# Attention and max-of-three MLP on one core: products with v held back until step 8, identity products in the first steps

## The chip, the cores and the metric

The kernel runs on one core of a Trainium2 chip. The core's engines work side by side, each through its own row of instructions, and wait for one another by semaphores: TensorE (PE in the profile) multiplies matrices, VectorE (DVE), ScalarE (ACT) and GpSimd (POOL) work on vectors, and SyncE (SP) issues DMAs. The metric is the device time of one execution in microseconds (us), as the median of several runs.

## The reference

Four batches of eight heads of attention, 576 positions of 64 values each, with a bias that a small network computes from the distance of two positions; the result goes through a layer that takes the maximum of three products and multiplies it by an output matrix.

```python
scores = scale * np.matmul(q, k.transpose(0, 1, 3, 2))
x = (psi_rel / psi_i)[..., None]
bias = np.maximum(x @ w1 + b1, 0.0) @ w2
scores = scores + bias.transpose(2, 0, 1)[None, :, :, :]
scores = scores - np.max(scores, axis=-1, keepdims=True)
attn = np.exp(scores)
attn = attn / (np.sum(attn, axis=-1, keepdims=True) + 1e-09)
attn_out = np.matmul(attn, v)
...
x = attn_out.transpose(0, 2, 1, 3).reshape(B * S, H * D)
h = np.maximum(np.maximum(x @ w1, x @ w2), x @ w3)
out = h @ w_out
```

## The kernel before

Three parts follow one another. The first (`bias_stage`) computes the bias for all heads and writes it to DRAM (`bias_d`). The second is attention, the third the max layer and its output (`moe`). The order of all instructions is that of the Python code (`manual_schedule`), with no scheduler behind it.

Attention runs over 16 units, each a pair of heads of one batch. A unit has NS = 5 steps, t = 0 to 4: four blocks of 128 query rows for two heads, and a last one that holds the left-over 64 rows of both heads. There are 80 steps, n = 0 to 79, and five more without a front that empty the pipeline (the drain). A step does the following, in this order:

- `front(n)`: PE multiplies q and k into the score banks s (L237). There are two such banks (tag "s", `bufs=2`), one for each head, so the next front waits for DVE's shifts of this one.
- the queue of products with v: `pvq` holds closures, and step t takes 1, 3, 2, 2 or 2 of them, if there are any (L348 to L350). This is the place of the change.
- `shift` and `expo`: DVE adds the bias and takes the minimum of the negated scores (sn and nm, L247; the last step of a unit uses the table biasm), ACT takes exponentials and their sums (e and sm, L259).
- `norm(n - 1)`: DVE's reciprocals of the sums of the step before (rc, L269), and POOL multiplies by them (L272).
- `prep`, at t = 0 and 1: ACT and POOL split q and k of the next unit (kh, kl, qh, ql).
- `split_x`: DVE writes a finished group of the attention's result out of PSUM, as xhi and xlo (L330, L331).
- `flip(n - 5)`: PE transposes the probabilities of five steps ago by products with an identity (tp at L291, the left-over columns into lp at L300); ACT (L369, L370) and DVE (L372) copy them to et.
- at t = 1 and t = 4 of the flipped step, `queue_pv` puts a group into the queue. It has five pairs of products (L320), one pair for each block of keys, the fifth with the tile vl, and sums into one PSUM bank (tag "pv", `bufs=1`). The group of t = 0 and 1 has 256 columns, that of t = 2 to 4 has 320.

The first pair of a group calls `split_x` for whatever is finished, and then writes to the same bank that the group before it used, so it has to wait until DVE has read that bank out.

The first group is put into the queue at the end of step 6, and the steps take from it as soon as there is something: two pairs at step 7, two at step 8, one at step 9. From then on each unit takes 1 and 3 pairs of a 320-column group at t = 0 and t = 1; at t = 2 its last pair and the first pair of a 256-column group; and 2 and 2 more of that group at t = 3 and t = 4. After the last step what is left in the queue is taken in one go (L529 and L530), and the third part begins.

Step 0 is issued at the end of the first part, while its last bias blocks are on their way; the loads of the last bias tables (`load_bias`, tile biasm at L161 to L163) stand in SP's row behind the stores of these blocks.

Of the kernel before, what the change touches and what calls it, by code (L numbers as in the profile page):

```python
# [9 lines left out]
F32 = mybir.dt.float32  # L10
# [9 lines left out]
def kernel(  # L20
# [12 lines left out]
    nc = tc.nc  # L33
# [13 lines left out]
    psum = ctx.enter_context(tc.tile_pool(name="psum", bufs=1, space=PSUM))  # L47
# [13 lines left out]
    ident = const.tile([128, 128], F32, name="ident")  # L61
# [95 lines left out]
    def load_bias(hp, t):  # L157
        if t < NTQ:
            nc.sync.dma_start(out=bias_t[t], in_=bias_rows(128 * t, 128, 2 * hp, 0, S, 2))
        else:  # L160
            nc.sync.dma_start(out=bias_t[t][0:LEFT], in_=bias_rows(LB, LEFT, 2 * hp, 0, S))  # L161
            nc.sync.dma_start(out=bias_t[t][64:64 + LEFT, 0:LB], in_=bias_rows(LB, LEFT, 2 * hp + 1, LEFT, LB))
            nc.sync.dma_start(out=bias_t[t][64:64 + LEFT, LB:S], in_=bias_rows(LB, LEFT, 2 * hp + 1, 0, LEFT))  # L163
# [4 lines left out]
    NS = NTQ + 1  # L168

    TS = 2  # L170
    sched = [(un, t) for un in range(len(units)) for t in range(NS)]
    NSTEP = len(sched)
    LAG = NS

    class Attention:
# [99 lines left out]
        def flip(self, n):  # L275
# [27 lines left out]
                nc.tensor.transpose(lp[0:64], e2[:, LB:S], ident)  # L303
            return tps, (el[:, c0:c0 + m], lp[:, 0:m])

        def queue_pv(self, un, c0, w0, ea, el):
            hp, b = units[un]
            u = self.data[un]
            made = []

            def pair(c):
                def run():
                    if c == 0:
                        self.split_x()
                        made.append(psum.tile([128, w0], F32, tag="pv", bufs=1, name=f"pv{un}_{c0}"))
                    pv = made[0]
                    for h in range(2):
                        p = slice(64 * h, 64 * h + 64)
                        w, x = (u["vt"][:, c, h], ea[:, c, h]) if c < NTQ else (u["vl"][:, h], el)
                        nc.tensor.matmul(pv[p], lhsT=w, rhs=x, start=(c == 0), stop=(c == NTQ))  # L320
                    if c == NTQ:
                        self.done.append((pv, hp, slice(b * S + c0, b * S + c0 + w0)))
                return run

            self.wait = True
            self.pvq.extend(pair(c) for c in range(NTQ + 1))
# [9 lines left out]
        def step(self, n, more=None):  # L336
            m, f = n - 1, n - LAG
            nh = 0
            if n < NSTEP:
                un, t = sched[n]  # L340
                hp, b = units[un]
                if t == 0 and un + 2 < len(units):
                    self.load_qk(un + 2)
                if t == 3 and un:
                    self.load_v(un)
                nh = self.heads(n)
                self.front(n)
            for _ in range((1, 3, 2, 2, 2)[n % NS]):  # L348
                if self.pvq:
                    self.pvq.pop(0)()  # L350
            back = 0 <= f < NSTEP
            for h in range(nh):
                self.shift(n, h)
                self.expo(n, h)
            if more is not None:
                next(more, None)
            if n < NSTEP and b == B - 1 and hp + 1 < HP:
                load_bias(hp + 1, t)
            if 0 <= m < NSTEP:
                self.norm(m)  # L360
            if n < NSTEP and un + 1 < len(units):
                if t == 0:
                    self.splits = self.prep(un + 1)
                if t < 2:
                    next(self.splits)
            self.split_x()
            if back:
                tps, left = self.flip(f)
                nc.scalar.copy(*tps[0])  # L369
                nc.scalar.copy(*left)  # L370
                if len(tps) > 1:
                    nc.vector.tensor_copy(*tps[1])  # L372
            if back:
                un, t = sched[f]
                g = 0 if t < TS else 1
                w = 128 * TS if g == 0 else S - 128 * TS
                del self.st[f]
                if t in (TS - 1, NS - 1):
                    self.queue_pv(un, 128 * TS * g, w, *self.et)
# [115 lines left out]
    with tc.manual_schedule():  # L495
        nc.vector.memset(signm, 0x80000000)
        warm = const.tile([128, 256], F32, name="warm")
# [6 lines left out]
        n = 0  # L504
# [87 lines left out]
```

## Time and profile before

| | us |
|---|---|
| median of 3 runs | 646.84 (646.67 to 647.37) |
| the profiled execution | 644.86 |
| its span, first to last instruction | 643.1 |
| PE busy in the span | 606.8 (94%) |
| DVE busy | 372.2 (58%) |
| ACT busy | 297.5 (46%) |
| POOL busy | 167.6 (26%) |

The bias part lasts until about 53 us, attention until about 344, the third part until the end. Busy time is a mean over these parts, so stretches are read by themselves: a table of windows gives the busy time of each engine and the clock that was granted to PE (PEclk, 1.00 is 2.4 GHz and 0.50 is 1.2 GHz). In a row of the order of time, the number in brackets is how long the engine stood idle before the instruction, and behind the arrow is what ended that. Where an instruction waits for nothing, the price of work in a row is read from one start to the next.

### The profile page before, as it was taken

How to read it: one execution, taken by the hardware profiler on the slowest of the kernel's cores; microseconds unless marked ns; L12 is line 12 of the kernel's file. 1: busy time of each engine (PE TensorE's matmuls, PEld its weight loads, DVE VectorE, ACT ScalarE, POOL GpSimd, SP SyncE). 2: the span in 40 equal slices, each digit the busy share in tenths (PEclk: the TensorE clock that was granted, in tenths of full speed). 3: DMA queues.
4: the chain of work that ended last, by engine and by line, in shares of the span. 5: the costliest groups of instructions: out<-in, count | busy, mean ns of one | idle time of the engine just before them, and what ended most of it. 6: DMA issues, size and time to landing. Idle time of an engine off the chain costs nothing.

```text
span 643.1 us, 11440 instructions
## 1 busy us (share of the span) xinstructions
PE 606.8 (94%) x4248; PEld 459.6 (71%) x4248; DVE 372.2 (58%) x942; ACT 297.5 (46%) x791; POOL 167.6 (26%) x189
## 2 busy tenths in 40 slices
PE   8997899999999999999989999999999999999998
PEld 4335666666666666666657898989889898988886
DVE  7993566667766766676644474646646473233331
ACT  7985767777777787777641000000000001034443
POOL 3403655555565556556320000000000000000000
PEclk9996799999999999999999999999999999999999
DMA  6978313621372235400001121212212110001111
GB/s 177 287 243 291 87 51 116 193 60 53 90 218 71 60 94 153 133 20 19 22 32 34 34 67 51 76 36 66 65 34 97 34 66 0 1 34 66 66 65 67
DMA packets 47863, 55.16 MB, mean 86 GB/s; under 512 B 21952, under 2 KB 31424, under 8 KB 47808
## 3 DMA queue, kind: packets, MB, share of 16 engines
q1 hardware_dynamic: 47808, 54.43, 27.4%
q8 instruction: 34, 0.56, 0.4%
q14 instruction: 21, 0.17, 0.1%
HBM read 38.81 MB, written 15.61 MB: 85 GB/s over the span
## 4 chain that ended last, share of the span: by engine, by line
PE 85%; ACT 5%; DVE 5%; issue 3%; DMA 2%; POOL 0%; DVEq 0%; ACTq 0%
PE pv L320 14%; PE s L237 12%; PE tp L291 11%; PE h L464 8%; PE h L466 8%; PE h L465 8%; PE g L464 4%; PE g L466 4%; PE g L465 4%; PE o L490 4%; PE o L489 4%; PE o L488 4%; ACT bs L144 2%; DMA bias_d<-bs 2%; DVE hid L106 1%
## 5 line engine op out<-in xcount | busy, mean ns | idle before, releaser
L259 ACT ACTIVATE e<-sn,nm 128x576 f32<-128x576 f32 x144 | 110.8, 771 | 71.5 <-DVE nm L247 66.0
L272 POOL TENSOR_SCALAR e<-e,rc 128x576 f32<-128x576 f32 x144 | 105.7, 747 | 92.6 <-PE tp L291 65.4
L471 ACT COPY m<-h 128x512 f32<-128x512 f32 (+1 forms) x30 | 16.3, 544 | 206.1 <-PE h L466 180.9
L247 DVE CUSTOM_DVE_ANT_0 sn<-s,bias 128x576 f32<-128x576 f32 x128 | 91.7, 753 | 34.2 <-PE s L237 34.2
L320 PE MATMUL pv<-et,vt 128*64 128x320 f32 (+1 forms) x512 | 79.4, 420 | 23.1 <-DVE xlo L331 20.2
L466 PE MATMUL h<-xhi,wl 128*128 128x512 f32 (+1 forms) x240 | 88.3, 368 | 0.0
L464 PE MATMUL h<-xhi,wh 128*128 128x512 f32 (+1 forms) x240 | 88.3, 368 | 0.0
L465 PE MATMUL h<-xlo,wh 128*128 128x512 f32 (+1 forms) x240 | 88.2, 368 | 0.0
L291 PEld LDWEIGHTS tp<-ident,e 128*128 128x128 f32 x576 | 62.3, 142 | 33.8 <-issue 30.3
L291 PE MATMUL tp<-ident,e 128*128 128x128 f32 x576 | 81.3, 282 | 0.0
L372 DVE COPY et<-tp 128x512 f32<-128x512 f32 x64 | 44.2, 690 | 42.7 <-PE tp L291 40.7
L320 PEld LDWEIGHTS pv<-et,vt 128*64 128x64 f32 x512 | 30.4, 136 | 52.5 <-issue 35.7
L237 PE MATMUL s<-kh,qh 64*128 64x288 f32 (+1 forms) x288 | 62.3, 359 | 3.9 <-DVE nm L247 2.8
L237 PE MATMUL s<-kl,qh 64*128 64x288 f32 (+1 forms) x288 | 52.8, 309 | 0.0
L237 PE MATMUL s<-kh,ql 64*128 64x288 f32 (+1 forms) x288 | 51.6, 303 | 0.0
L369 ACT COPY et<-tp 128x512 f32<-128x512 f32 x80 | 45.8, 573 | 9.1 <-PE tp L291 9.1
L464 PEld LDWEIGHTS h<-xhi,wh 128*128 128x128 f32 x240 | 45.1, 188 | 6.2 <-issue 0.5
L443 DVE TENSOR_TENSOR hl<-ht,hh 128x128 fp32r<-128x128 f32 x108 | 23.4, 285 | 44.9 <-ACT hh L442 44.9
L465 PEld LDWEIGHTS h<-xlo,wh 128*128 128x128 f32 x240 | 45.0, 188 | 5.8
L466 PEld LDWEIGHTS h<-xhi,wl 128*128 128x128 f32 x240 | 45.0, 188 | 5.7
L472 DVE TENSOR_TENSOR m<-h,m 128x512 f32<-128x512 f32 (+1 forms) x30 | 19.1, 637 | 51.3 <-ACT m L471 51.3
L206 POOL TENSOR_TENSOR kl<-kr,kh 128x640 fp32r<-128x640 f32 x16 | 32.5, 2034 | 58.7 <-ACT kh L205 58.7
(77 smaller groups left out, 1051.5 us busy)
## 6 DMA issues: line engine op xcount, KB each, us to landing
bias_d<-bs SPq DMA_DIRECT2D x36, 295.5 KB, 5.0
bias<-bias_d SPq DMA_DIRECT2D x16, 576.0 KB, 4.0
w<-in_moe_w_dram SPq DMA_DIRECT2D x18, 512.0 KB, 3.5
qr<-in_qd_dram SPq DMA_DIRECT2D x16, 320.0 KB, 3.6
kr<-in_kd_dram SPq DMA_DIRECT2D x16, 320.0 KB, 3.8
out_dram<-ot SPq DMA_DIRECT2D x17, 256.0 KB, 2.0
vt<-in_v_dram SPq DMA_DIRECT2D x32, 128.0 KB, 2.5
w64o<-in_moe_w_out_dram SPq DMA_DIRECT2D x6, 512.0 KB, 3.2
```

Of the source, the lines that this page charges most:

```text
L206: nc.gpsimd.tensor_tensor(out=lo, in0=r, in1=hi.bitcast(F32), op=ALU.subtract)
L237: nc.tensor.matmul(ss[h][:, x, 0:HALF], lhsT=u[q][p, r], rhs=u[k][p, c:c + HALF], start=(j == 0), stop=(j == 2))
L247: nc.vector.tensor_tensor_reduce(out=sn.rearrange("p (a b) -> p a b", a=2), in0=st["s"][h][:, :, 0:HALF], in1=bt.rearrange("p (a b) -> p a ...
L259: nc.scalar.activation(st["e"][:, S * h:S * h + S], sn, ACTF.Exp, scale=-1.0, bias=nm, accum_out=st["sm"][:, h:h + 1])
L272: nc.gpsimd.tensor_scalar(out=e, in0=e, scalar1=rc[:, h:h + 1], scalar2=1.0, op0=ALU.mult, op1=ALU.mult)
L291: nc.tensor.transpose(tp[:, 128 * c:128 * c + 128], e2[:, k0:k0 + 128], ident)
L320: nc.tensor.matmul(pv[p], lhsT=w, rhs=x, start=(c == 0), stop=(c == NTQ))
L369: nc.scalar.copy(*tps[0])
L372: nc.vector.tensor_copy(*tps[1])
L464: nc.tensor.matmul(o, lhsT=hi[:, r], rhs=x, start=(c == 0), stop=False)
L465: nc.tensor.matmul(o, lhsT=hi[:, r], rhs=y, start=False, stop=False)
L466: nc.tensor.matmul(o, lhsT=lo[:, r], rhs=x, start=False, stop=(c == KDM - 1))
```

## The change

A pair is taken from the queue only from step n = LAG + TS + 1 = 8 on (LAG is 5, TS is 2). The steps 0 to 4 get a new method, `warm`, behind the front: four products of the identity with itself, 128 x 128, into the bank of lp, which nothing reads. Nothing else changes; the numbers 1, 3, 2, 2, 2 stay.

```diff
+        def warm(self, n):
+            w = psum.tile([128, 128], F32, tag="l", bufs=1, name=f"warm{n}")
+            for _ in range(4):
+                nc.tensor.matmul(w, lhsT=ident, rhs=ident, start=True, stop=True)
+
         def queue_pv(self, un, c0, w0, ea, el):
...
                 nh = self.heads(n)
                 self.front(n)
+            if n < NS:
+                self.warm(n)
             for _ in range((1, 3, 2, 2, 2)[n % NS]):
-                if self.pvq:
+                if self.pvq and n >= LAG + TS + 1:
                     self.pvq.pop(0)()
```

In the rows of order below, a line number of after is larger by 5 to 8 than that of before (L326 is L320, L336 and L337 are L330 and L331, L380 is L372).

PE, step 17 (t = 2 of the fourth unit), from the end of the front to the flip; pv_256 is the group of 320 columns, pv_0 the one of 256. Before:

```order
L237 MATMUL s_2_0_1639<-kh_1315,ql_1371 128x288
L237 MATMUL s_2_1_1640<-kh_1315,ql_1371 128x288
L320 MATMUL pv_256_1546<-et_1_1425,vl_82 64x320 x2
L320 MATMUL pv_0_1657<-et_0_1568,vt_1441 64x256 x2
L291 MATMUL tp_2_0_1677<-ident,e_1413 128x128 x4
L291 MATMUL tp_2_1_1682<-ident,e_1413 128x128 x4
L300 MATMUL lp_2_1687<-ident,e_1413 128x128
```

And after:

```order
L237 MATMUL s_2_0_1662<-kh_1335,ql_1394 128x288
L237 MATMUL s_2_1_1663<-kh_1335,ql_1394 128x288
L326 MATMUL pv_256_1620<-et_1_1447,vt_1215 64x320 x2
L326 MATMUL pv_256_1620<-et_1_1447,vl_82 64x320 x2
L291 MATMUL tp_2_0_1699<-ident,e_1433 128x128 x4
L291 MATMUL tp_2_1_1704<-ident,e_1433 128x128 x4
L300 MATMUL lp_2_1709<-ident,e_1433 128x128
```

The step now takes the last two pairs of one group; the first pair of the next group has moved to step 18, and DVE's split of this group from before the shifts of this step to behind them.

DVE, step 15 (t = 0 of the same unit), from the shift of the second head to the first shift of step 16. Before:

```order
L247 ISA sn_1_1555,nm_1_1556<-s_0_1_1533,bias_85 128x576
L247 ISA nm_1_1556 128x1
L269 RECIPROCAL rc_1561<-sm_1509 128x1
L372 COPY et_0_1568<-tp_0_1_1574 128x4x128
L247 ISA sn_0_1604,nm_0_1605<-s_1_0_1584,bias_86 128x576
```

And after:

```order
L247 ISA sn_1_1575,nm_1_1576<-s_0_1_1554,bias_85 128x576
L247 ISA nm_1_1576 128x1
L269 RECIPROCAL rc_1581<-sm_1532 128x1
L336 CAST xhi_933<-pv_0_1482 128x256
L337 TENSOR_TENSOR xlo_937<-pv_0_1482,xhi_933 128x256
L380 COPY et_0_1590<-tp_0_1_1596 128x4x128
L247 ISA sn_0_1627,nm_0_1628<-s_1_0_1606,bias_86 128x576
```

The split of the 256-column group, which stood at the end of step 14, now stands between the reciprocal and the copy of et of step 15.

PE, from the end of the front of step 0 to the start of that of step 1. Before:

```order
L237 MATMUL s_0_0_889<-kh_238,ql_303 128x288
L237 MATMUL s_0_1_890<-kh_238,ql_303 128x288
L237 MATMUL s_1_0_936<-kh_238,qh_302 128x288
L237 MATMUL s_1_1_937<-kh_238,qh_302 128x288
L237 MATMUL s_1_0_936<-kl_239,qh_302 128x288
```

And after:

```order
L237 MATMUL s_0_0_889<-kh_238,ql_303 128x288
L237 MATMUL s_0_1_890<-kh_238,ql_303 128x288
L310 MATMUL warm_903<-ident 128x128 x4
L237 MATMUL s_1_0_941<-kh_238,qh_302 128x288
L237 MATMUL s_1_1_942<-kh_238,qh_302 128x288
L237 MATMUL s_1_0_941<-kl_239,qh_302 128x288
```

Four identity products stand between the two fronts, where PE waits for the shifts of step 0.

## Rows read from the trace of the kernel before

**Rows 1.** Windows: stretch; busy us (instructions) by engine, PEclk, DMA share, GB/s.

```profile
54.00:73.00 19.00, 15.96 (x84) 12.40 (x82) 9.06 (x28) 12.29 (x32) 9.78 (x12) 0.50 0.65 200
73.50:74.00 0.50, 0.50 (x7) 0.50 (x6) 0.42 (x1) 0.00 (x0) 0.50 (x1) 1.00 0.00 0
95.00:112.27 17.27, 15.92 (x137) 10.95 (x137) 11.43 (x32) 12.69 (x35) 9.69 (x11) 1.00 0.40 117
345.00:600.00 255.00, 255.00 (x1226) 223.86 (x1225) 127.98 (x263) 32.30 (x96) 0.00 (x0) 1.00 0.15 49
```

**Rows 2.** PE's waits: who waited for whom, us, times, longest.

```profile
PE pv L320 <- DVE xlo L331: 20.2, 15, 1.3
...
PE pv L320 <- ACT et L369: 2.9, 5, 1.3
```

**Rows 3.** Timeline of PE: start us, us, instructions [idle before <-releaser].

```profile
103.45 0.76 PE L320 MATMUL pv<-et,vt 128*64 128x320 f32 x4
104.14 1.09 PE L291 MATMUL tp<-ident,e 128*128 128x128 f32 x8
...
105.27 0.40 PE L237 MATMUL s<-kh,qh 64*128 64x288 f32 x2
...
106.27 1.83 PE L320 MATMUL pv<-et,vt 128*64 128x320 f32 x12
108.03 1.09 PE L291 MATMUL tp<-ident,e 128*128 128x128 f32 x8
...
110.16 0.76 PE L320 MATMUL pv<-et,vl 128*64 128x320 f32 x4
112.27 0.65 PE L320 MATMUL pv<-et,vt 128*64 128x256 f32 x4 [1.35 <-DVE xlo L331]
112.85 1.09 PE L291 MATMUL tp<-ident,e 128*128 128x128 f32 x8
...
114.97 1.08 PE L320 MATMUL pv<-et,vt 128*64 128x256 f32 x8
115.98 1.09 PE L291 MATMUL tp<-ident,e 128*128 128x128 f32 x8
```

**Rows 4.** Timeline of DVE around a step t=0.

```profile
101.80 0.42 DVE L330 CAST xhi<-pv 128x256 fp32r<-128x256 f32 x1 [0.21 <-PE pv L320]
102.26 0.42 DVE L331 TENSOR_TENSOR xlo<-pv,xhi 128x256 fp32r<-128x256 f32 x1
...
104.92 0.16 DVE L269 RECIPROCAL rc<-sm 128x1 f32<-128x1 f32 x1
105.27 0.69 DVE L372 COPY et<-tp 128x512 f32<-128x512 f32 x1 [0.20 <-PE tp L291]
```

**Rows 5.** Timeline of PE in the fill.

```profile
62.12 1.28 PE L237 MATMUL s<-kh,qh 64*128 64x288 f32 x2 [0.63 <-DVE nm L247]
...
67.89 0.61 PE L237 MATMUL s<-kh,qh 64*128 64x288 f32 x1 [0.32 <-DVE nm L247]
...
69.63 1.97 PE L291 MATMUL tp<-ident,e 128*128 128x128 f32 x8
...
77.45 1.15 PE L320 MATMUL pv<-et,vt 128*64 128x256 f32 x8 [1.31 <-ACT et L369]
```

**Rows 6.** Timeline of DVE: the shift of step 4.

```profile
67.07 0.76 DVE L247 CUSTOM_DVE_ANT_0 sn<-s,biasm 128x576 f32<-128x576 f32 x1 [1.15 <-PE s L237]
```

**Rows 7.** Tile biasm, 50 to 75 us: its last load, and all its landings.

```profile
L163 SPq DMA_DIRECT2D biasm<-bias_d x1: 596/596/596, 64.0 to 64.0; - x1
...
DMA to landing us min/median/max: 2.8/3.3/3.4
```

**Rows 8.** Timeline of PE: the five products at the program's start.

```profile
1.22 4.38 PE L501 MATMUL wps<-warm 128*128 128x256 f32 x10 [1.22 <-DVE warm L498]
```

**Rows 9.** Timeline of PE in the drain.

```profile
334.68 0.65 PE L320 MATMUL pv<-et,vt 128*64 128x256 f32 x4 [1.32 <-DVE xlo L331]
...
340.89 2.37 PE L320 MATMUL pv<-et,vt 128*64 128x320 f32 x16 [0.46 <-ACT et L369]
```

## The prediction

> **What bounds the kernel now.** I read the windows by stage first. From 345 to 600 us, in the second half of the program, TensorE (PE) is busy all 255 of 255 us, so what ends earlier before it ends the kernel earlier. In one unit of the attention part, 95.00 to 112.27, PE is busy 15.92 of 17.27 us, ScalarE (ACT) 12.69, VectorE (DVE) 11.43 and GpSimd (POOL) 9.69: PE is the bound there too, and idle for 1.35 us a unit [rows 1]. The list of waits names that idle time: PE's product with v waits for DVE's xlo 15 times, 20.2 us in all [rows 2]. The order of time shows where: at 112.27, in the step t=2 of a unit, the first pair of a new group stands behind the last pair of the old one, and both use the one pv bank, which DVE has to empty by xhi and xlo in between [rows 3]. The other meeting of a unit, from t=4 to t=0, has no such wait: 103.45 has no idle time before it. Last I read the fill, 53 to 75 us, where PE goes through the first fronts with gaps (0.63 us before the front at 62.12 [rows 5]) and at a granted clock of 0.50, the 1.2 GHz level, until 73.5 [rows 1].
>
> **The change part by part.** Held until step 8, the queue is one pair behind for good. A group now ends with one pair at t=0 and with two pairs at t=2, and the next one starts in the step after, on the other side of a flip and a front.
>
> *The steady units.* Steps are priced by starts in [rows 3]. One pair of 320 columns takes 104.14 - 103.45 = 0.69; three take 108.03 - 106.27 = 1.76, so 0.535 for each further pair. Two pairs of 256 take 115.98 - 114.97 = 1.01, one of them 112.85 - 112.27 = 0.58. The meeting step takes 112.85 - 110.16 = 2.69. Before, a unit's five steps are 0.69 + 1.76 + 2.69 + 1.01 + 1.01 = 7.16 us of products with v. After, they are 0.58 (one of 256) + 1.76 + 1.225 (two of 320) + 1.01 + 1.01 = 5.59. That is **1.57 us a unit**: the wait of 1.35 and 0.22 for a start of a group that is saved. There are 15 such waits, one of them in the drain, so 14 x 1.57 = **21.9 us**.
>
> Two splits now stand at the end of their steps in DVE's row, ahead of the copy of et; what is behind them is that copy and the next step's shifts. At t=2 the last pair ends after 1.225 us of products, the split takes 1.0 us more, and flip and front (1.13 + 1.0) lie between it and the next pair: 0.7 us to spare. At t=0 it is tight. DVE's reciprocal ends at about 105.05, the split of 256 columns takes 0.46 + 0.42 = 0.88 [rows 4], and the first pair of t=1 would come at about 106.15, some 0.1 before 106.27, since the pair of t=0 is shorter: about 0.2 us to spare. The copy of et moves from 105.27 to 105.95, and the shift of t=1, which waits for a front that ends near 106.3, to some 0.3 later; the front of t=2, which needs that shift, is not before 109.0 (106.15 + 1.76 + 1.13). So I cost both splits at nothing; if the cover is gone, each 0.1 us costs 1.4 us over 14 units. ACT's 12.69 and DVE's 11.43 us fit into a unit of 15.7 us [rows 1]. SyncE's (SP) loads of v wait for the same pair of t=2 as before, and no queue gets a new entry.
>
> *The fill.* 20 identity products are added, four behind each of the fronts 0 to 4. No row of before shows one. From above: a product of 256 columns takes 2 x 4.38 / 10 = 0.88 us [rows 8], so 0.44 for 128 columns; from below: a transpose of 128 columns takes about 0.22 in the half-rate stretch (1.97 for eight with their tail [rows 5]). Four are 0.9 to 1.75 us at the low clock and half of that at the high one. I take 1.7 and 0.85, since these products are two rows each like those of [rows 8]. At the low clock they fill the place in which PE waits for two shifts of DVE (0.76 each [rows 6]), and PE has no gap left from the first front on. Before the clock rose at 73.5, PE had its last gap at 67.9; so I take it to rise in the second or third front. What does this bring? Not the fronts 1 to 3, which are then paced by the shifts. Nor step 4: the last load of its table biasm is issued by SP at 64.0 and lands 2.8 us later, at about 66.8 [rows 7], and its shift starts at 67.07 now [rows 6], so at most 0.3 us are to be had there. Behind that, 67.9 to 73.5 is PE work at half rate: 5.6 us that take 2.8 at full rate. After that ACT's chain of exponentials and copies holds the flips, which is why PE waits 1.31 at 77.45 [rows 5]; with no product in step 7 that wait and the products' 1.15 us fall away there, and the gain is kept. I put the fill at 0.2 + 2.8 = **3.0 us**. Its ends: 4.4, if biasm doesn't hold and the shifts alone pace the steps (1.4 us more), and a loss of 1.0, if the clock stays low until 73.5: 1.7 us then stand in a wait of two shifts, 1.5, in four steps and of one shift in the fifth, 0.2 to 0.3 over in each of the four and 0.9 in the fifth, and the products that left step 7 give 1.15 back.
>
> *A rule against it.* The flips' transposes stood in the stretch in which the clock rose: eight from 69.63 [rows 5], and at 73.5 the granted clock is 1.00 [rows 1]. The Trainium skill, page "TensorE: Matmul & The Clock Gate", section "Part 4: PE-mode transpose", says that the full clock doesn't engage for transposes, as they don't count as a busy TensorE in the same way. If products with an identity were treated as such, the added ones would not bring the clock up, and the sum would be that with a loss of 1.0 us in the fill; the trace speaks against it, as transposes were over a third of the stretch from 67.9 to the rise.
>
> *The drain.* Three waits there go: 1.32 at 334.68, 0.46 at 340.89 [rows 9], and of the five waits for ACT's et [rows 2], 2.9 us, the three small ones, 1.1 together. New: with no front between steps a flip of 1.13 us covers the 1.32 from a last pair to the next first one but for 0.2 and 0.1, and in the last drain nothing covers it (1.2 for 256 columns). One pair more stands there (0.43). Net 2.9 - 1.5 - 0.4 = **1.0 us** gained.
>
> *Sum.* 21.9 + 3.0 + 1.0 = 25.9 us. The profiled execution took 644.86 us (span 643.1), so it would be 619.0. It lies 2.0 us below the median of the runs, 646.84; from that the same sum gives 620.9, and I predict **621.0**.
>
> **The rivals.**
> - *The clock doesn't come up earlier* (the products count for nothing, or the first fronts still leave gaps). For it: from 54 to 73 us PE is busy 15.96 of 19 us at 0.50 without a rise [rows 1]. Against: the gaps go. 646.84 - 21.9 - 1.0 + 1.0 = 625 us.
> - *Part of the wait comes back at t=0 to t=1.* DVE's split there has only 0.2 us to spare, behind a reciprocal that waits for ACT's sums. At 0.5 us a unit it is 7 us: 628 us. Against: at 104.92 the reciprocal follows the shift with no idle time [rows 4].
> - *Slower than before*: the same place, if the reciprocal ahead of the split waited for ACT so long that PE's first pair of t=1 came over 1.85 us late in every unit (25.9 / 14). At 2.0 us that is 28 us lost against 25.9 gained: 649 us. ACT's row would have to slip by over 2 us there in every unit, and it has 15.7 - 12.7 = 3.0 us of a unit free. Very unlikely.
> - *No change to be told*: the same with 1.75 to 1.95 us.
>
> **How the numbers follow.** The forecast has a chance of 0.75, the low clock 0.14, the partial wait 0.07, slower 0.02, no change 0.02. The range begins where the fill brings 4.4 and the measurement stands as far below the median as the profiled run: 619.0 - 1.4 = 617.6, so 617.5. It ends past the low clock's 625 with 0.1 us a unit of lost cover (1.4): 626.5. That leaves out about 0.12. A difference of 0.2%, 1.3 us, is about what a measurement can tell from no change: faster by more 0.96, within it 0.02, slower by more 0.02.
>
> **What would show it.** Right: the wait of pv for xlo is gone from the steady units and stands once, at the end of the attention part; a unit takes 15.7 us and PE is busy in nearly all of it; the clock rises near 60 us; DVE's shift of step 4 starts near 67 with its idle time put down to a DMA; the second half starts about 26 us earlier. Wrong: a wait of pv for xlo at the first pair of t=1, idle time before DVE's reciprocals, or a half-rate stretch as long as before.

## The result, and the profile after

The changed kernel takes 621.07 us (median of 4 runs, 619.95 to 623.03) against 646.75 of before beside it; the ratio is 0.9609 with a 95% interval of 0.9579 to 0.9639. Run again beside other runs of before it took 621.37 against 646.27, a ratio of 0.9619 (0.9604 to 0.9633). The profiled execution is the longest of its group, 623.03 us with a span of 621.2.

The page of the profiled execution: busy time of the engines, and PE's busy tenths and granted clock in 40 slices of the span.

```profile
PE 603.8 (97%) x4288; PEld 462.0 (74%) x4288; DVE 367.5 (59%) x942; ACT 297.6 (48%) x791; POOL 168.0 (27%) x189
...
PE   8979799999999999999999999999999999999997
...
PEclk9989799999999999999999999999999999999999
```

PE is now busy for 97% of the span. The clock's row shows a dip in the third slice and another in the fifth, which holds 62 to 78 us; [rows 1] had the level 0.50 for all of 54 to 73 us.

The windows of five stretches (stretch; busy us and instructions of PE, PEld, DVE, ACT, POOL; PEclk, DMA share, GB/s): the first steps of the fill, what follows them, one unit, and a stretch of the third part as long as that of [rows 1].

```profile
56.00:66.00 10.00, 10.00 (x85) 8.33 (x82) 6.01 (x19) 8.30 (x21) 6.44 (x7) 1.00 0.73 240
66.00:70.60 4.60, 0.78 (x6) 0.45 (x4) 0.76 (x3) 0.23 (x2) 0.97 (x2) 0.82 0.62 160
70.60:75.80 5.20, 5.14 (x30) 4.53 (x32) 2.29 (x8) 3.77 (x10) 2.37 (x4) 0.50 0.40 114
88.13:103.82 15.69, 15.69 (x139) 10.98 (x137) 11.03 (x32) 12.69 (x35) 9.71 (x11) 1.00 0.22 63
323.00:578.00 255.00, 255.00 (x1227) 223.81 (x1226) 127.93 (x262) 32.14 (x95) 0.00 (x0) 1.00 0.15 49
```

One unit takes 15.69 us, all of it busy, against 17.27 in [rows 1]; from 80.15 us to 319.02 PE has no idle time at all. The first steps run at full clock without a gap. Then PE is busy for only 0.78 of 4.6 us, and the 5.2 us after that run at 0.50.

PE's waits, largest of the attention part:

```profile
PE s L237 <- DVE nm L247: 3.9, 1, 3.9
...
PE pv L326 <- DVE xlo L337: 1.1, 1, 1.1
PE tp L291 <- ACT et L377: 0.8, 1, 0.8
```

The 15 waits of [rows 2] for xlo are one, 1.1 us, at the end of the attention part. In their place stands a single wait of 3.9 us of a front for DVE.

The order of time of PE in the unit that answers to [rows 3] (start us, us, instructions): a step t=0 with one pair, t=1 with three, t=2 with two.

```profile
103.24 0.65 PE L326 MATMUL pv<-et,vl 128*64 128x256 f32 x4
103.82 1.09 PE L291 MATMUL tp<-ident,e 128*128 128x128 f32 x8
...
104.95 0.40 PE L237 MATMUL s<-kh,qh 64*128 64x288 f32 x2
...
105.94 1.84 PE L326 MATMUL pv<-et,vt 128*64 128x320 f32 x12
107.71 1.09 PE L291 MATMUL tp<-ident,e 128*128 128x128 f32 x8
...
109.84 0.76 PE L326 MATMUL pv<-et,vt 128*64 128x320 f32 x4
110.42 0.71 PE L326 MATMUL pv<-et,vl 128*64 128x320 f32 x4
111.06 1.09 PE L291 MATMUL tp<-ident,e 128*128 128x128 f32 x8
```

No row has idle time in front. The three steps cost 103.82 - 103.24 = 0.58, 107.71 - 105.94 = 1.77 and 111.06 - 109.84 = 1.22 us of products with v.

And DVE in the step t=0, which answers to [rows 4]:

```profile
104.70 0.16 DVE L269 RECIPROCAL rc<-sm 128x1 f32<-128x1 f32 x1
104.78 0.41 DVE L336 CAST xhi<-pv 128x256 fp32r<-128x256 f32 x1
105.22 0.42 DVE L337 TENSOR_TENSOR xlo<-pv,xhi 128x256 fp32r<-128x256 f32 x1
105.56 0.68 DVE L380 COPY et<-tp 128x512 f32<-128x512 f32 x1
106.16 0.75 DVE L247 CUSTOM_DVE_ANT_0 sn<-s,bias 128x576 f32<-128x576 f32 x1
```

The split runs back to back with the reciprocal, and xlo ends at about 105.64, 0.3 us ahead of the first pair of t=1 at 105.94. The shift of t=1, at 106.16, follows the copy of et without idle time.

The fill, first PE and then DVE, which answer to [rows 5] and [rows 6]:

```profile
63.62 1.16 PE L310 MATMUL warm<-ident 128*128 128x128 f32 x8
64.53 0.38 PE L237 MATMUL s<-kh,qh 128*128 128x288 f32 x1
...
65.40 1.05 PE L310 MATMUL warm<-ident 128*128 128x128 f32 x8
66.39 0.40 PE L237 MATMUL s<-kh,qh 64*128 64x288 f32 x1
70.66 0.61 PE L237 MATMUL s<-kh,qh 64*128 64x288 f32 x1 [3.88 <-DVE nm L247]
...
72.40 1.97 PE L291 MATMUL tp<-ident,e 128*128 128x128 f32 x8
```

```profile
69.84 0.76 DVE L247 CUSTOM_DVE_ANT_0 sn<-s,biasm 128x576 f32<-128x576 f32 x1 [4.72 <-DMA biasm<-bias_d]
```

The products (L310, eight rows a step) fill the gaps between the fronts. After the fifth group PE has one matmul to do and then waits 3.88 us for the shift of step 4, and that shift has waited 4.72 us for the DMA of biasm. The transposes at 72.40 take 1.97 us, the half-rate value of [rows 5].

The tile biasm in this stretch, which answers to [rows 7]: its last load is issued 3.2 us later than in the profiled execution of before.

```profile
L163 SPq DMA_DIRECT2D biasm<-bias_d x1: 596/596/596, 67.2 to 67.2; - x1
...
DMA to landing us min/median/max: 2.5/3.6/3.7
```

The end of the attention part on PE, which answers to [rows 9]:

```profile
317.26 0.65 PE L326 MATMUL pv<-et,vl 128*64 128x256 f32 x4
319.02 2.37 PE L326 MATMUL pv<-et,vt 128*64 128x320 f32 x16 [1.10 <-DVE xlo L337]
...
321.86 0.50 PE L472 MATMUL h<-xhi,wh 128*128 128x512 f32 x1
```

### The profile page after: what moved, and what is told of

Read it like the earlier page. It is cut to its first block, busy times and chain, and to the rows that moved or that the text cites. A ratio compares the mean times of both kernels' runs of the same rounds, so it can differ in the third digit from the quotient of the medians.

```text
span 621.2 us, 11560 instructions
## 1 busy us (share of the span) xinstructions
PE 603.8 (97%) x4288; PEld 462.0 (74%) x4288; DVE 367.5 (59%) x942; ACT 297.6 (48%) x791; POOL 168.0 (27%) x189
## 4 chain that ended last, share of the span: by engine, by line
PE 89%; ACT 4%; DMA 3%; DVE 3%; issue 1%; SPq 0%; ACTq 0%; DVEq 0%
PE pv L326 14%; PE tp L291 12%; PE s L237 12%; PE h L472 8%; PE h L473 8%; PE h L474 8%; PE g L473 4%; PE g L474 4%; PE g L472 4%; PE o L497 4%; PE o L496 4%; PE o L498 4%; DVE hid L106 2%; ACT bs L144 2%; DMA bias_d<-bs 2%; PE bp L127 2%
## 5 line engine op out<-in xcount | busy, mean ns | idle before, releaser
L272 POOL TENSOR_SCALAR e<-e,rc 128x576 f32<-128x576 f32 x144 | 105.7, 748 | 72.3 <-DVE rc L269 26.2
L326 PE MATMUL pv<-et,vt 128*64 128x320 f32 (+1 forms) x512 | 76.0, 418 | 1.1 <-DVE xlo L337 1.1
L237 PE MATMUL s<-kh,qh 64*128 64x288 f32 (+1 forms) x288 | 59.0, 347 | 4.5 <-DVE nm L247 3.9
L380 DVE COPY et<-tp 128x512 f32<-128x512 f32 x64 | 43.9, 686 | 27.0 <-PE tp L291 26.4
L237 PE MATMUL s<-kl,qh 64*128 64x288 f32 (+1 forms) x288 | 50.0, 298 | 0.0
L326 PEld LDWEIGHTS pv<-et,vt 128*64 128x64 f32 x512 | 31.5, 136 | 24.5 <-issue 11.4
L127 PE MATMUL bp<-hid,w2s 128*32 128x79 f32 (+48 forms) x640 | 42.8, 402 | 6.5 <-ACT bs L144 4.4
L237 PE MATMUL s<-kh,ql 64*128 64x288 f32 (+1 forms) x288 | 49.0, 293 | 0.0
```

Source lines behind the costliest of these rows:

```text
L127: nc.tensor.matmul(bp[32 * c:32 * c + 32, o:o + w], lhsT=w2s, rhs=src, start=True, stop=True)
L237: nc.tensor.matmul(ss[h][:, x, 0:HALF], lhsT=u[q][p, r], rhs=u[k][p, c:c + HALF], start=(j == 0), stop=(j == 2))
L272: nc.gpsimd.tensor_scalar(out=e, in0=e, scalar1=rc[:, h:h + 1], scalar2=1.0, op0=ALU.mult, op1=ALU.mult)
```

## The experiments

All diffs are against the changed kernel, and each ratio is to the kernel before in the same group of runs.

### Only the queue is held

```diff
-            if n < NS:
-                self.warm(n)
```

> The changed kernel without its identity products; only the queue is held until step 8. My theory (the steady units carry the gain: 14 x 1.57 us, the drain 1.0, and in the fill the products taken out of step 7 some 1.2, the identity products the rest of it, 1.8): about 24 us faster than before, 622.8, with the clock at the low level from about 53 to 73 us as before. Rival (the identity products bring nothing, since the load of the table biasm paces the fill): as the changed kernel, 621.1.

Measured: 620.66 us against 645.38, ratio 0.9619 (0.9601 to 0.9637). That is the changed kernel's ratio. The clock is at the low level in the fill as before; the window from 58.5 to 75.5 us, and DVE's shift of step 4 (the clock fell here at about 58.4 us, in the profile of before at 53):

```profile
58.50:75.50 17.00, 14.13 (x73) 10.96 (x71) 8.22 (x25) 11.37 (x31) 10.95 (x12) 0.50 0.65 202
```

```profile
68.39 0.76 DVE L247 CUSTOM_DVE_ANT_0 sn<-s,biasm 128x576 f32<-128x576 f32 x1 [1.66 <-DMA biasm<-bias_d]
```

Here too step 4 waits for biasm, for 1.66 us. The rival holds: the held queue alone gives the whole gain, as far as intervals of 0.2 to 0.3% either way can tell.

### Only the identity products

```diff
-                if self.pvq and n >= LAG + TS + 1:
+                if self.pvq:
```

> The changed kernel with the queue taken from as before (nothing is held), only the identity products are added. My theory: the waits of pv for xlo stay (15, 20.2 us), the clock stays up in the first steps, and the gain is at most the 2 to 3 us of the fill: 644 to 645. Rival (they bring nothing): 646.7. Should the identity products carry more than that, the sum for the steady units is wrong.

Measured: 645.34 us against 645.38, ratio 1.000 (0.9987 to 1.0013). The products do to the clock in the first steps what was expected, and nothing to the time. PE's waits, and the windows of the fill:

```profile
PE pv L326 <- DVE xlo L337: 20.2, 15, 1.3
...
PE pv L326 <- ACT et L377: 2.9, 5, 1.3
```

```profile
56.00:70.00 14.00, 11.43 (x94) 9.43 (x94) 6.62 (x20) 8.55 (x22) 7.41 (x8) 1.00 0.69 222
71.60:75.00 3.40, 3.40 (x22) 2.79 (x21) 1.96 (x7) 2.98 (x8) 1.40 (x3) 0.50 0.20 43
```

The steps run at full clock up to 70 us, against 0.50 before, and the time is the same; the waits are those of [rows 2]. Here too step 4 waits for biasm, for 3.63 us, its shift begins at 69.39, and the clock falls at about 71.6. Of the expectation the gain of up to 2 to 3 us was wrong; the rival came.

### The split behind the flip

```diff
-            self.split_x()
             if back:
                 tps, left = self.flip(f)
...
                     nc.vector.tensor_copy(*tps[1])
+            self.split_x()
```

> The changed kernel with the split of a finished group moved in DVE's row from ahead of the copy of et to behind it, so that it waits for the flip. My theory: the next step's first pair then comes some 0.75 us too early for the split at t=0 to t=1 and some 0.85 us at t=2 to t=3, 1.6 us in each of 14 units, about 22 us: back to 642 to 645. Rival (there is more to spare than the rows say, or PE has other slack): 621 to 625.

Measured: 642.75 us against 645.38, ratio 0.9962 (0.9946 to 0.9978): some 22 us of the 25 are lost again. PE and then DVE in one unit:

```profile
104.54 1.09 PE L291 MATMUL tp<-ident,e 128*128 128x128 f32 x8
...
107.30 1.83 PE L326 MATMUL pv<-et,vt 128*64 128x320 f32 x12 [0.56 <-DVE xlo L337]
...
112.42 1.09 PE L291 MATMUL tp<-ident,e 128*128 128x128 f32 x8
...
115.27 1.08 PE L326 MATMUL pv<-et,vt 128*64 128x256 f32 x8 [0.66 <-PE s L237]
```

```profile
105.67 0.69 DVE L379 COPY et<-tp 128x512 f32<-128x512 f32 x1
106.28 0.42 DVE L336 CAST xhi<-pv 128x256 fp32r<-128x256 f32 x1
106.73 0.42 DVE L337 TENSOR_TENSOR xlo<-pv,xhi 128x256 fp32r<-128x256 f32 x1
...
113.55 0.69 DVE L379 COPY et<-tp 128x512 f32<-128x512 f32 x1 [0.74 <-PE tp L291]
114.16 0.48 DVE L336 CAST xhi<-pv 128x320 fp32r<-128x320 f32 x1
114.67 0.49 DVE L337 TENSOR_TENSOR xlo<-pv,xhi 128x320 fp32r<-128x320 f32 x1
```

At both meetings the split stands behind the copy of et, which at the second one waits 0.74 us for the flip; xlo ends at 107.15 and 115.16, and PE waits 0.56 and 0.66 us. The second wait is put down to the front, which had long ended; what ended last is xlo at 115.16, 0.1 us ahead of the product. A unit takes 17.05 us (90.25 to 107.30 on PE's row of the waiting pair), 1.36 longer than the changed kernel's; 1.22 of that are the two waits, and the cause of the remaining 0.14 is open. Over 14 units 1.36 is 19.0 us; another 3.3 are lost in the drain, where PE takes 21.73 us from the front of step 79 to the third part (321.82 to 343.55) against 18.46 in the changed kernel. So it is not that groups meet in different steps that carries the gain, but that DVE empties the bank under the cover of a flip and a front.

### The load of a bias table behind the last stores

```diff
-                if g in (10, 18, 26, 34):
+                if g in (10, 18, 26):
                     load_bias(0, g // 8 - 1)
                 if g >= NG:
+                    load_bias(0, 3)
```

> The changed kernel with the load of the bias table of step 3 moved in SP's row from ahead of the last three stores of bias blocks to behind them, so that these stores, and with them the load of biasm that waits for their landing, go out about 4 us earlier. My theory (biasm sets step 4 in the fill, and where its wait is long, the clock falls in it): the wait of DVE for biasm goes, the clock stays up through the fill, 618 to 619.5. Rival (the fill is paced by the shifts and by ACT, and biasm is only one of several): 621.

Measured: 619.03 us against 645.38, ratio 0.9599 (0.9582 to 0.9615), by the ratios some 1.3 us under the version that only holds (0.9619) and 0.6 to 1.3 us under the changed kernel (0.9609 and 0.9619). biasm's loads went out at 60.2 to 61.3 us, but took 5.7 to 6.4 us to land, and step 4's shift began at 67.20; its idle time of 1.50 us is put down to PE, so that it waited for biasm is likely and not shown. The clock was at 0.50 from about 54.8 to 58.2 us and at 1.00 from there to 80. The intervals of the ratios overlap, so of the theory the direction is only likely; the last three runs, in which more loads move, settle it.

### The changed kernel again

> The changed kernel again, beside the same runs of before as the others of this group. Theory from the first four: it stands within 1 us of the one that only holds (620.7), since the identity products bring nothing while biasm comes late; its ratio is 0.960 to 0.963. Rival: it is some 2 us faster than that one, as the sum had it.

Measured: 621.37 us against 646.27, ratio 0.9619 (0.9604 to 0.9633), the same as the version that only holds. In its profile, too, step 4 waits for biasm (4.38 us, until 68.62), PE stands idle for 3.54 us until 69.44, and the clock falls in that wait, at about 69.3. Here it was back at 72.7 us.

### The table load later, without products

The two diffs together, of the first and the fourth experiment.

> Queue held, table load of step 3 behind the stores as in e4, but no identity products. Theory: with biasm out of the way the low clock in the fill has its price, so this is 1.5 to 3 us slower than e4's 619.0, at 620.5 to 622. Rival (the products are worth nothing here either): 619.

Measured: 621.34 us against 646.27, ratio 0.9618 (0.9605 to 0.9631), 0.0019 above the one with products. The moved load alone brings nothing; that it brings a little with the products is likely and not shown, since the two intervals overlap. Step 4 still waits for biasm here, for 1.60 us, until 68.80.

### Transposes in place of the products

```diff
-            for _ in range(4):
-                nc.tensor.matmul(w, lhsT=ident, rhs=ident, start=True, stop=True)
+            for _ in range(8):
+                nc.tensor.transpose(w, ident, ident)
```

with the table load as in the fourth experiment.

> As e4, but each group of four identity products is eight transposes of the identity, which take as many rows of 128 columns. If transposes don't count as a busy TensorE, the clock stays at the low level for some 17 us in the fill and the time is that of e6 (620.5 to 622). If they do, it is that of e4 (619.0), with the clock up in the first steps.

Measured: 620.55 us against 646.27, ratio 0.9605 (0.9587 to 0.9624), which by itself fits either. The clock decides it. The windows of the fill with transposes, and then of the version with neither (the run ahead):

```profile
56.00:65.00 9.00, 8.49 (x72) 6.45 (x69) 4.48 (x14) 6.70 (x17) 5.46 (x6) 1.00 0.95 296
```

```profile
60.40:73.90 13.50, 11.30 (x55) 8.77 (x57) 6.52 (x22) 8.88 (x25) 9.56 (x11) 0.50 0.67 190
```

With transposes the clock stays at 1.00 through the first steps, and on to 80 us; with neither it is at 0.50 from 60.4 to 73.9. In these profiles, one of each, transposes keep the clock up as the products do.

### Both loads out of biasm's way, and one pair more in the drain

```diff
-                if t == 0 and un + 2 < len(units):
+                if t == 0 and 0 < un and un + 2 < len(units):
                     self.load_qk(un + 2)
...
-            for _ in range((1, 3, 2, 2, 2)[n % NS]):
+            for _ in range((1, 3, 2, 2, 2)[n % NS] + (n == NSTEP + LAG - 1)):
...
             load_bias(0, NTQ)
+            at.load_qk(2)
```

with the table load as in the fourth experiment.

> As e4, with the loads of q and k for the third unit moved in SP's row from ahead of the loads of biasm to behind them, and one pair more taken in the last step of the drain, so that the flip covers DVE's last split. Theory: biasm lands about 2 us earlier and step 4 with it (1.5 to 2 us), and the last wait of 1.1 us for xlo goes but for 0.3 (0.8 us): 616 to 617. Rival (step 4 is then set by the shifts, and the drain by ACT's copies): 618 to 619.

Measured: 617.01 us against 646.27, ratio 0.9552 (0.9538 to 0.9566): faster than the changed kernel of the same group by 4.4 us. Step 4's shift began at 66.17 with no wait for biasm, and of the wait for xlo at the end a wait of 0.46 us for ACT's copy is left. The drain gives 0.80 of the 4.4: from the front of step 79 to the third part PE takes 17.66 us (298.22 to 315.88) against 18.46.

### The same without products, and the same again

> The kernel of e8 without its identity products. Theory: with both loads out of the way, the half-rate stretch of the fill has its full price, the 2.8 us of the prediction less what ACT's chain holds back: 618.5 to 620, its ratio to before at least 0.0025 above e8's 0.9552. Rival (the products bring nothing here either): 617, a ratio within 0.001 of e8's.

> e8 again, beside the same runs of before as e9: 617.0, ratio 0.955.

Measured: 619.76 us without products, ratio 0.9602 (0.9581 to 0.9623), and 616.29 us with them, ratio 0.9543 (0.9526 to 0.9561), both against 645.81. The windows from 60 to 70 us, without and then with:

```profile
60.00:70.00 10.00, 8.35 (x44) 6.46 (x41) 4.61 (x16) 6.13 (x17) 7.92 (x10) 0.50 0.78 239
```

```profile
60.00:70.00 10.00, 9.85 (x87) 8.30 (x87) 6.51 (x22) 8.35 (x22) 8.55 (x11) 1.00 0.75 217
```

Here, where no load holds step 4 back, the products are worth 3.5 us by the medians, and the intervals of the two ratios don't meet. The profiled executions differ by 2.6 us: 0.9 stands between the shifts of step 0 and step 4 (55.68 to 66.84 against 55.72 to 65.94), and 1.7 between those of step 4 and step 13 (66.84 to 94.76 against 65.94 to 92.20). The version with both loads moved, the drain's pair and the products, 616.3 to 617.0 us, is the fastest of the study.

## Why the prediction was right, and where it was not

**What bounds the kernel.** Right. All that ended earlier before 344 us ended the kernel earlier: the third part took 299.3 us from its first product at 343.73 and from that at 321.86.

**The steady units.** Right: 15.69 us a unit where 15.7 was forecast, 1.58 saved where it was 1.57. Its prices by starts held at 0.58, 1.77 and 1.22 us. The spare time at t=0 was 0.3 us where 0.2 was forecast, at t=2 0.8 (xlo's end at 112.37 to the pair at 113.18) for 0.7; that this cover carries the gain was shown by the split behind the flip, which used it up and lost some 22 us.

**The drain.** Right: from the front of step 79 to the first product of the third part PE took 19.4 us before (324.32 to 343.73) and 18.5 after (303.40 to 321.86), 0.95 gained where 1.0 was forecast, with a last wait of 1.1 us for 1.2.

**The fill.** This term was mis-sized: 3.0 us forecast. From the shift of step 4 to that of step 13, 30.74 us in the profiled execution of before (67.07 to 97.81) became 27.92 with the held queue alone (68.39 to 96.31) and 27.77 in the changed kernel (69.84 to 97.61). Of that 1.57 is the first steady saving; the rest, 1.25 and 1.40, is about what the products taken out of step 7 were to give. In the second profile of the changed kernel, where the clock came back earlier, it was 26.94 (68.62 to 95.56), so 2.23. The identity products gave the time nothing: the ratios with and without them are the same, and alone they gave 1.000. What they gave behind step 4 in that second profile was lost ahead of it: the shift of step 4 came 13.64 and 13.30 us after that of step 0 in the changed kernel (56.20 to 69.84, 55.32 to 68.62), and 12.04 with the held queue alone (56.35 to 68.39).

The step of this term that failed is the one that says the work behind step 4 runs at full rate. It had the reason in hand, that step 4 cannot start before biasm lands, and did not ask what PE does until then: with its products done early it stands idle for 3.5 to 3.9 us, and in both profiles of the changed kernel the clock falls in that wait, so that the work behind it starts at half rate again. Nor was 66.8 us, read from one execution, a safe time for biasm: step 4's shift began at 68.39 to 69.84 in five other profiles with that order of loads (the changed kernel twice, and the first three experiments).

With the loads moved out of the way the products brought 3.5 us, near the 3.0 that the prediction gave to the fill, but not where it put them: of the 2.6 in the profiled executions 0.9 stands ahead of step 4, where 0.2 was forecast, and 1.7 behind it, where 2.8 was. In four profiles with the clock up behind step 4 (the table load moved, the transposes, and both of the version with both loads moved) it is 26.2 to 26.3 us from its shift to that of step 13; in the four that stay at the low level until 73.6 to 75.8 it is 27.4 to 27.9. Nor was the gain all kept, as the prediction had it: with products and loads moved PE waits twice for ACT's copies of et behind step 4, 0.76 and 0.70 us, and without products once, 0.82. So the mechanism is there, and a DMA stood in front of it.

**The price of the products.** Four were put at 0.85 us at full clock; from 56.22 to 57.30 in the first step they took 1.08. It lay under DVE's shifts either way.

**The sum.** 25.9 us were forecast; the two runs of the changed kernel show 25.7 and 24.9, and the one that only holds 24.7. (14 x 1.57 is 22.0, not 21.9; that slip is 0.1 us.) That the time of 621.07 met the 621.0 so closely is in part luck: a fill that was 0.8 to 1.8 us too large stood against a base, 646.84, that was high, as other runs of before have medians of 645.4 to 646.3; and the interval of the ratio leaves 23.3 to 27.2 us for the gain.

**The rivals.** The low clock's rival, 625 us, did not come as it was put: the clock was up from the first step and fell in the wait for biasm, where the low level met the work behind step 4 and not the products. The partial wait at t=0 did not come, and so neither did the rivals that start from it. The rule of the Trainium skill, page "TensorE: Matmul & The Clock Gate", section "Part 4: PE-mode transpose", that transposes don't bring TensorE to its full clock, is not borne out as far as holding the clock goes: with transposes in the gaps between the fronts the granted clock was 1.00 from 56 to 65 us, with fronts alone it was at 0.50 from 60.4 us on.

**What would show it.** The waits and the unit came as described. The third part started 21.9 us earlier in this execution, not 26: the shift of step 4 alone came 2.8 us later than in the profile of before. Its wait for the DMA came too, but until 69.84, not near 67. The clock did not rise near 60: it had not fallen by then. Of the signs of being wrong none came: no pair of t=1 waits for xlo, the only wait before a reciprocal (1.22 us at 306.54) stands in the drain, and the half-rate stretch was some 7 us long instead of 20.

## What to carry to other kernels

Where one engine has to empty a bank that the bound engine needs next, put the two uses on either side of other work of the bound engine, and check in the emptying engine's row what stands ahead of it there: here 0.3 us of spare time at t=0 and 0.8 at t=2 carried some 22 of the 25 us. Products that only keep the clock up paid nothing here while a load paced the same steps; look first for what the steps would wait for once they are faster, move that, and then the clock is worth its price. And price a term that rests on one landing time from several executions.

## What the hardware showed that was not expected

The clock kept up by filler work fell in the first long wait behind it: it was at 1.00 from 56 to 66 us with PE busy throughout, PE then stood idle for 3.88 us, and the clock fell at about 69 us, to come back only at 75.8. And the issue of one load can take longer on SP's row with no change to that load: in all four profiles that have the identity products and the loads in the old order, one of the three loads of biasm took 1.24 to 1.50 us there; in the two without products, and in the six with loads moved, each took 0.60 or less. Whether the products cause it no run shows; if they do, part of what they bring is lost ahead of step 4 by it.
